# Attention with adaLN and a mixer MLP on one core: scores computed transposed, the MLP put among attention, all engines in a listed order

## The chip, the cores and the metric

One core of one Trainium2 chip. The metric is the device time of one execution in microseconds (us), the slowest core's, of which there is one here. Several executions are timed, and the median is compared.

## What is computed

```python
def reference(A_x, A_k_cache, A_v_cache, A_wq, A_wo, B_x, B_w1, B_w2, B_w3, B_w4, c, w_mod):
    def _A_ref(x, k_cache, v_cache, wq, wo):      # 2048 queries, D = 640, 32 heads of 128, 2048 keys
        q = (x @ wq).reshape(B, Sq, H, Dh).transpose(0, 2, 1, 3)
        scores = jnp.einsum('bhqd,bhkd->bhqk', q, k_cache) * Dh ** (-0.5)
        p = _softmax(scores, axis=-1)
        o = jnp.einsum('bhqk,bhkd->bhqd', p, v_cache)
        return o.transpose(0, 2, 1, 3).reshape(B, Sq, H * Dh) @ wo
    def _B_ref(x, w1, w2, w3, w4):                # F = 1728
        h = _gelu(_layernorm(x) @ w1)
        ...                                       # the four quarters of h shifted by +1, -1, +2, -2 rows: hs
        x1 = x + hs @ w2
        return x1 + _gelu(_layernorm(x1) @ w3) @ w4
    sa, ca, ga, sb, cb, gb = six parts of _silu(c) @ w_mod
    h = _layernorm(x) * (1 + ca) + sa
    x = x + ga * _A_ref(h, ...)
    h = _layernorm(x) * (1 + cb) + sb
    return x + gb * _B_ref(h, ...)
```

All tensors are bfloat16; sums are kept in float32.

## The kernel before

The five engines are called PE (matmul), ACT (activation functions), DVE (elementwise), POOL and SP; SP and POOL also issue DMAs. The kernel is a row of blocks, one after the other. The first (lines 96 to 179) loads `w_mod` and all of `x`, computes the six modulation vectors, normalizes 16 tiles of 128 queries and leaves `hT`, the transposed input of attention.

The second is attention. It runs over heads, and in each head over 16 query tiles; one (head, tile) is a group, 512 in all. PE computes a group's scores in two halves of 1024 keys, queries on the partitions, into `Sps` (L327). DVE scales each half into `negS` in SBUF and takes its row minimum of the negated scores in the same instruction (L371). POOL joins the two minima (L270), and ACT computes exp over 2048 keys with that as bias (L399) into `Pb`. For the product with V the probabilities must stand with keys on the partitions: seven of eight groups are transposed by a DMA from SP (L297), the eighth by PE (L312) with copies by DVE (L363). Six groups later PE multiplies them with V, whose 129th column is ones and yields the row sum (L344). DVE takes its reciprocal (L382), ACT scales (L405), and POOL writes the 128x128 result to `o_scratch` in DRAM (L285). The next head's K tiles are transposed on PE (L228) and its queries projected (L233) as small jobs in fixed slots, with ACT copying out (L241, L244). The order on each engine is that of these loops, and blocking waits on semaphores tie them together.

Behind attention come four blocks in which attention is over: the output projection with the residual and two layer norms (L487 and L525 to L539, `OTj` read back from `o_scratch` by transposing DMAs, L471), the first MLP layer with GELU (L585, L600), the second with a layer norm (L618 to L641), and the third and fourth (L678, L701, L690, L709 to L714). Layer norms take their root on ACT (L435).

Of the kernel before, what the change touches and what calls it, by code (L numbers as in the profile page):

```python
# [1 line left out]

# [4 lines left out]
ACT = mybir.ActivationFunctionType  # L7
BF16 = mybir.dt.bfloat16
F32 = mybir.dt.float32


class Ev:

    def __init__(self, nc, es, name):
        self.sem = es.enter_context(nc.semaphore(name))
        self.n = 0
# [9 lines left out]
        eng.wait_ge(ev.sem, val)  # L26


def bass_adaLN_cond__mha_block_cached__mixer_s_mlp__prompt_kernel(
    nc, A_x, A_k_cache, A_v_cache, A_wq, A_wo, B_x, B_w1, B_w2, B_w3, B_w4, c, w_mod, out,  # L30
):
# [12 lines left out]
    EPS = 1e-5  # L44
    NG = H * NQT
    x2d = A_x[0]
    out2d = out[0]
    HD = D // 2
    NC2 = [(0, 512), (512, D - 512)]

    with ExitStack() as es:
        sb = lambda name, shape, dt: es.enter_context(nc.sbuf_tensor(name, shape, dt))
        ps = lambda name, shape, dt: es.enter_context(nc.psum_tensor(name, shape, dt))
        o_scr = nc.dram_tensor("o_scratch", [NQT, 128, H, DH], BF16)
        ident = sb("ident", [128, 128], BF16)
# [13 lines left out]
        with ExitStack() as esA:  # L69
            sbA = lambda name, shape, dt: esA.enter_context(nc.sbuf_tensor(name, shape, dt))  # L70
            hT = sbA("hT", [128, KT, SQ], BF16)
            with ExitStack() as es0:
                sb0 = lambda name, shape, dt: es0.enter_context(nc.sbuf_tensor(name, shape, dt))
                c_sb = sb0("c_sb", [128, KT], BF16)
                c_f = sb0("c_f", [128, KT], F32)
                s_bc = sb0("s_bc", [128, KT, 128], BF16)
# [3 lines left out]
                st = sb0("st", [128, 2, 12], F32)  # L80
                mv = sb0("mv", [128, 2, 2], F32)
# [3 lines left out]
                hA = sb0("hA", [128, 2, D], BF16)  # L85
                block = es0.enter_context(nc.Block())
# [92 lines left out]
            with ExitStack() as es1:  # L179
# [10 lines left out]
                On = sb1("On", [128, 8, 128], BF16)  # L190
# [3 lines left out]
                rl = sb1("rl", [128, 8], F32)  # L194
# [3 lines left out]
                block = es1.enter_context(nc.Block())  # L198
# [213 lines left out]
        with ExitStack() as es2:  # L412
            sb2 = lambda name, shape, dt: es2.enter_context(nc.sbuf_tensor(name, shape, dt))
            x1 = sb2("x1", [128, NQT, D], BF16)
# [300 lines left out]
                        W(v, e_o, e_o.n)  # L715


# [1 line left out]
_INS = ['A_x', 'A_k_cache', 'A_v_cache', 'A_wq', 'A_wo', 'B_x', 'B_w1', 'B_w2', 'B_w3', 'B_w4', 'c', 'w_mod']  # L719
_OUTS = [((1, 2048, 640), 'bfloat16')]  # L720
# [23 lines left out]
```

## Time and profile before

| | us |
|---|---|
| three timed runs | 2002.43, 2003.85, 2011.81 |
| median | 2003.85 |
| span of the profiled execution | 2008.4 |
| PE busy in it | 1587.3 (79%) |
| DVE busy | 1547.8 (77%) |
| ACT busy | 1374.8 (68%) |
| POOL busy | 662.8 (33%) |

The profiled execution's own device time is not recorded beside its span; the span lies within the three timed runs, and the program has no part before or behind it that the trace shows. Mean granted clock of PE was 0.954 of full speed. In the profile an engine's group of instructions stands with its line, the tile written and the tiles read, the shape, the count, its busy time and mean time, and the idle time of the engine just before these instructions with what ended it. PE's matmuls are pipelined, so a mean of 387 ns for 512 columns is a latency, and rates are read from dense chains.

### The profile page before, as it was taken

To read this page: it belongs to the slowest core of one execution; us is meant where nothing else is said; L and a number is where in the kernel's file an instruction comes from. 1 tells how busy PE (TensorE), PEld (TensorE's weight loads), DVE (VectorE), ACT (ScalarE), POOL (GpSimd) and SP (SyncE) were. 2 spreads that over 40 slices of the span, in tenths; PEclk is the share of its full clock that TensorE was granted. 3 is DMA by queue.
4 is the path that set the end of the run, shared out by engine and by line. 5 is a ranking of instruction groups with operands and counts; after the bars stand their busy time and mean duration, and the time that the engine had idled before them with its cause. 6 is when DMAs were issued, how large, how long until landed. Compare 5 with 4: busy or idle time off the path is not lost. (4 is left out here: it accounts for less than half of the span.)

```text
span 2008.4 us, 39142 instructions
## 1 busy us (share of the span) xinstructions
PE 1587.3 (79%) x14480; PEld 993.0 (49%) x14708; DVE 1547.8 (77%) x3151; ACT 1374.8 (68%) x1428; POOL 662.8 (33%) x1321
## 2 busy tenths in 40 slices
PE   2388888888888888888888888888888469966798
PEld 1145555555555555555555555555555335533344
DVE  5588888898889888888888888888988437737025
ACT  1288888888888888888888888888888401143430
POOL 0224444444444444444444444444443200010000
PEclk7589999999999999999999999999999879989899
DMA  4189999999999989999988989999999775510201
GB/s 150 38 160 201 198 198 199 201 198 195 199 202 204 190 197 199 198 201 199 194 188 191 187 200 196 203 199 196 195 202 196 174 199 122 106 33 1 89 14 40
DMA packets 1044381, 333.95 MB, mean 166 GB/s; under 512 B 1011744, under 2 KB 1024992, under 8 KB 1044192
## 3 DMA queue, kind: packets, MB, share of 16 engines
q1 hardware_dynamic: 1013472, 275.81, 68.3%
q0 software_dynamic: 30720, 55.63, 10.6%
q8 instruction: 118, 1.93, 0.4%
q14 instruction: 71, 0.58, 0.1%
HBM read 60.26 MB, written 19.40 MB: 40 GB/s over the span
## 5 line engine op out<-in xcount | busy, mean ns | idle before, releaser
L371 DVE TENSOR_SCALAR_CACHE_REDUCE negS<-Sps 128x1024 f32<-128x1024 f32 x1024 | 1207.7, 1217 | 168.6 <-PE Sps L327 163.7
L399 ACT ACTIVATE Pb<-negS,nm 128x2048 bf16<-128x2048 f32 x512 | 1025.2, 2003 | 213.9 <-POOL nm L270 194.8
L327 PE MATMUL Sps<-KTs,QT 128*128 128x512 bf16 x1889 | 549.8, 387 | 162.7 <-DVE negS L371 142.2
L270 POOL TENSOR_SCALAR nm<-nm 128x1 f32<-128x1 f32 x512 | 145.3, 284 | 840.9 <-DVE negS L371 840.9
L327 PEld LDWEIGHTS Sps<-KTs,QT 128*128 128x128 bf16 x2048 | 154.3, 98 | 402.8 <-DVE negS L371 320.6
L344 PEld LDWEIGHTS PTp<-Vaug,PTs 128*128 128x128 bf16 x4096 | 263.0, 99 | 66.4 <-issue 24.0
L285 POOL DMA_DIRECT2D o_scratch<-On x512 | 289.3, 565 | 4.5 <-ACT On L405 4.0
L344 PEld LDWEIGHTS Oaug<-Vaug,PTs 128*128 128x128 bf16 x4096 | 259.6, 98 | 59.9 <-issue 1.1
L344 PE MATMUL PTp<-Vaug,PTs 128*128 128x129 bf16 x4096 | 286.9, 223 | 1.5 <-ACT On L405 1.2
L344 PE MATMUL Oaug<-Vaug,PTs 128*128 128x129 bf16 x4096 | 281.4, 220 | 0.0
L487 PE MATMUL Sps<-wo,OTj 128*128 128x128 bf16 (+1 forms) x1008 | 140.9, 301 | 38.6 <-DMA OTj<-o_scratch 37.8
L233 PE MATMUL QPp<-hT,wq 128*128 128x512 bf16 x607 | 155.9, 386 | 5.2 <-ACT QT L244 2.0
L487 PEld LDWEIGHTS Sps<-wo,OTj 128*128 128x128 bf16 x1024 | 80.1, 99 | 100.1 <-DMA OTj<-o_scratch 37.6
L435 ACT ACTIVATE sdB<-mvB 128x1 f32<-128x1 f32 x48 | 9.7, 203 | 158.3 <-DVE mvB L67 158.3
L312 PE MATMUL PTp<-ident,Pb 128*128 128x128 bf16 x1024 | 78.7, 220 | 43.3 <-ACT Pb L399 43.3
L256 POOL DMA_DIRECT2D Vaug<-in_A_v_cache_dram x128 | 104.9, 820 | 5.6 <-issue 5.5
L363 DVE COPY PTs<-PTp 128x1024 bf16<-128x1024 bf16 x128 | 86.8, 678 | 25.4 <-PE PTp L312 25.3
L250 POOL DMA_DIRECT2D Knat<-in_A_k_cache_dram x128 | 104.7, 820 | 0.4 <-issue 0.4
L709 DVE TENSOR_TENSOR t<-Sps,xb 128x640 f32<-128x640 f32 x16 | 13.2, 825 | 103.6 <-PE Sps L690 103.6
L405 ACT ACTIVATE On<-Oaug,rl 128x128 bf16<-128x128 f32 x256 | 89.7, 350 | 2.5 <-DVE rl L382 2.5
L405 ACT ACTIVATE On<-PTp,rl 128x128 bf16<-128x128 f32 x256 | 89.5, 350 | 2.0 <-DVE rl L382 2.0
L312 PEld LDWEIGHTS PTp<-ident,Pb 128*128 128x128 bf16 x1024 | 60.1, 98 | 54.6 <-ACT Pb L399 54.5
(72 smaller groups left out, 1127.6 us busy)
## 6 DMA issues: line engine op xcount, KB each, us to landing
Knat<-in_A_k_cache_dram POOLq DMA_DIRECT2D x128, 128.0 KB, 3.7
Vaug<-in_A_v_cache_dram POOLq DMA_DIRECT2D x128, 128.0 KB, 3.8
o_scratch<-On POOLq DMA_DIRECT2D x512, 32.0 KB, 3.3
PTs<-Pb SPq DMA_TRANSPOSE x448, 4.8
wq<-in_A_wq_dram POOLq DMA_DIRECT2D x32, 160.0 KB, 4.7
wo<-in_A_wo_dram SPq DMA_DIRECT2D x1, 5120.0 KB, 17.0
wmod<-in_w_mod_dram SPq DMA_DIRECT2D x1, 4800.0 KB, 14.8
x_sb<-in_A_x_dram SPq DMA_DIRECT2D x1, 2560.0 KB, 21.3
```

What stands on the lines that cost most here:

```text
L233: ins = t.matmul(QPp[:, 0:512], wq[:, hb, kk, :], hT[:, kk, cc * 512:(cc + 1) * 512], start=(kk == 0), stop=(kk == KT - 1))
L250: e_k[hb][pc // 2].inc(e.dma_start(Knat[:, hb, pc * 4:(pc + 1) * 4, :], A_k_cache[0, h, pc * 512:(pc + 1) * 512, :].rearrange("(t p) d -> ...
L256: e_v[hb].inc(e.dma_start(Vaug[:, hb, q * 4:(q + 1) * 4, 0:128], A_v_cache[0, h, q * 512:(q + 1) * 512, :].rearrange("(t p) d -> p t d", p ...
L270: e_nm.inc(g.tensor_scalar(out=nm[:, r8:r8 + 1], in0=nm0[:, r8:r8 + 1], scalar1=nm1[:, r8:r8 + 1], scalar2=None, op0=ALU.min))
L285: e_od[g_ % 8].inc(g.dma_start(o_scr[jj, :, hh, :], On[:, g_ % 8, :]), 16)
L312: ins = t.transpose(PTp[:, q * 128:(q + 1) * 128], Pb[:, b4, kt * 128:(kt + 1) * 128], ident[:])
L327: ins = t.matmul(Sps[:, col:col + 512], QT[:, hb, j * 128:(j + 1) * 128], KTs[:, hb, col:col + 512], start=True, stop=True)
L344: ins = t.matmul(ob[:, 0:129], PTs[:, b4, kt, :], Vaug[:, hb, kt, 0:129], start=(kt == 0), stop=(kt == NKT - 1))
L371: ins = v.tensor_scalar(out=negS[:, b, half * 1024:(half + 1) * 1024], in0=Sps[:, half * 1024:(half + 1) * 1024], scalar1=-SCALE, scalar2= ...
L399: e_exp.inc(a.activation(Pb[:, b4, :], negS[:, b, :], ACT.Exp, bias=nm[:, r8:r8 + 1], scale=-1.0))
L405: e_nrm.inc(a.activation(On[:, r8, :], OB[g_ % NOB][:, 0:128], ACT.Copy, scale=rl[:, r8:r8 + 1]))
L487: ins = t.matmul(YB[b][:, c0:c0 + cw], OTj[:, jj % 3, hh, :], wo[:, hh, c0:c0 + cw], start=(hh == 0), stop=(hh == H - 1))
```

## The change

The kernel is written anew as a list of operations (`fast_path`), each with an engine, a supposed duration, a priority and the tiles that it reads and writes. `Plan.schedule` puts them in order by a list scheduler with these durations: of those that can start soonest on an engine (within 30 ns) it takes the one with the lowest priority number. `Plan.emit` writes out the order with semaphore waits. The durations do not know of table loads of ACT, which are put into the program afterwards wherever the next function is not in the loaded set.

The queries are cut into 4 chunks of 512. The outer loop runs over chunks, the inner over 32 heads; one (chunk, head) is a step, 128 in all. In a step the scores are computed transposed, keys on the partitions and 512 queries along the row, two key tiles to one PSUM tile `S` of 1024 columns, of which there are two. ACT computes exp from PSUM without a maximum, straight into `PT`, which is already the operand that PV needs. PV accumulates four query tiles in two PSUM banks, `O0` and `O1`, one tile of each. DVE normalizes into `On`, and every four heads four small transposing DMAs and eight matmul groups add the output projection into `y_t`. K is loaded from DRAM by a transposing DMA. The MLP of a chunk (`phase_b`) is put among the steps of the next chunk; that of the last chunk comes behind everything. All small products share two PSUM tiles `M`. At the end the reciprocals of the row sums are compared with two bounds; if one is outside, the old kernel (`general_path`, word for word the one before) runs as well.

```diff
+    def schedule(self):
...
+                lim = min(st)[0] + 30.0
+                c = min((x for x in st if x[0] <= lim), key=lambda x: x[1:3])
+                if best is None or c[0] < best[0]:
+                    best = c
...
+def fast_path(nc, es, flag, A_x, A_k_cache, A_v_cache, A_wq, A_wo, B_w1, B_w2, B_w3, B_w4, c, w_mod, out):
...
+    S_ps = [ps("S%d" % i, [128, 1024]) for i in range(2)]
+    O_ps = [ps("O%d" % i, [128, 512]) for i in range(2)]
+    M_ps = [ps("M%d" % i, [128, 512]) for i in range(2)]
...
+    EXPSET = "natural_log_exp_and_others"
+    P.op("ACT", lambda e: e.preload_act_table_set(EXPSET), 1300, (), (), -200)
+
+    def back_to_exp(g, prio):
+        o = P.op("ACT", lambda e: e.preload_act_table_set(EXPSET), 1300, (), (), prio, after=tuple(g))
+        return (o,)
...
+    def ln(src, src_tiles, prio):
...
+        P.op("ACT", lambda e: e.activation(rs[i].ap, mv[i][:, 1:2], ACT.Ln, bias=EPS), 220, (mv[i],), (rs[i],), prio - 50)
+        P.op("ACT", lambda e: e.activation(rs[i].ap, rs[i].ap, ACT.Exp, scale=-0.5), 220, (rs[i],), (rs[i],), prio - 50)
...
+    def step(ch, h):
+        s = ch * H + h
+        k, v, w, q = KTs[s % 2], V[s % 2], wq[s % 2], QT[s % 2]
...
+        dma("SP", lambda e: e.dma_start_transpose(k.ap.unsqueeze(1), A_k_cache[0, h]), 700, (), (k,), lp)
+        dma("POOL", lambda e: e.dma_start(w.ap, A_wq[:, h * 128:(h + 1) * 128].rearrange("(k p) d -> p k d", p=128)), 160, (), (w,), lp - 0.5)
+        dma("POOL", lambda e: e.dma_start(v[:, :, 0:128], A_v_cache[0, h].rearrange("(t p) d -> p t d", p=128)), 512, (), (v,), lp + 0.2)
...
+        P.op("PE", qp, KT * MM(QC), (w,) + tuple(hT[ch % 2]), (m,), s - 1.8)
...
+        for j in range(NKT // 2):
...
+            P.op("PE", smm, 2 * MM(QC), (k, q), (sp,), s + j / 8 - 1.0)
+            last_exp[s, j] = P.op("ACT", lambda e, sp=sp, pt=pt: e.activation(
+                pt.ap.rearrange("p k q -> p (k q)"), sp.ap, ACT.Exp, scale=SCALE), 1040, (sp,), (pt,), s + j / 8,
+                after=gate.pop((s, j), ()))
+            for b in range(2):
...
+                P.op("PE", pv, 4 * 59, (pt, v), (o[b],), s + j / 8 - 0.9 + b * 0.01, accum=True)
...
+    def phase_b(ch):
...
+        X1, X2 = base + 5, base + 13
+        a1 = () if last else (lambda: last_exp[X1, 7],)
...
+            P.op("PE", mm, KT * MM(QC), (WA,) + tuple(nT[0:4]), (m,), X1 - 1, after=a1)
+            for (p0, p1, dl) in segs[n]:
+                g1.append(P.op("ACT", lambda e, m=m, n=n, p0=p0, p1=p1, dl=dl: e.activation(
+                    us_t[p0:p1, n, 128 + dl:640 + dl], m[p0:p1, :], GELU), act(QC), (m,), (us,), X1 - 2, after=a1))
+        if not last:
+            gate[X1 + 1, 0] = back_to_exp(g1, X1 - 2)
...
+            plan.schedule()
+            plan.emit(nc, es, {"SP": 24, "POOL": 12})
+        redo = nc.values_load(flag[0:1, 0:1])
+        with nc.If(redo > 0):
+            general_path(nc, A_x, A_k_cache, A_v_cache, A_wq, A_wo, B_x, B_w1, B_w2, B_w3, B_w4, c, w_mod, out)
```

PE, in the middle of attention. Before, a group's four score matmuls (L327) alternate with 16 matmuls of PV of an earlier group (L344, into `PTp` or `Oaug` in turn), with eight transposes (L312) now and then:

```order
L344 MATMUL Oaug<-Vaug,PTs 128x129 x16
L327 MATMUL Sps<-KTs,QT 128x512 x4
L344 MATMUL PTp<-Vaug,PTs 128x129 x16
L312 MATMUL PTp<-ident,Pb 128x128 x8
L327 MATMUL Sps<-KTs,QT 128x512 x4
```

After, at a change of step in a stretch without output projection (L470 is PV, L458 the scores, L446 the q projection of the step after next):

```order
L470 MATMUL f_O<-f_V,f_PT 128x129 x8
L458 MATMUL f_S<-f_QT,f_KTs 128x512 x2
L446 MATMUL f_M<-f_hT,f_wq 128x512 x5
L470 MATMUL f_O<-f_V,f_PT 128x129 x8
L458 MATMUL f_S<-f_QT,f_KTs 128x512 x4
L470 MATMUL f_O<-f_V,f_PT 128x129 x16
L458 MATMUL f_S<-f_QT,f_KTs 128x512 x2
L470 MATMUL f_O<-f_V,f_PT 128x129 x8
L458 MATMUL f_S<-f_QT,f_KTs 128x512 x2
```

The eight PV matmuls of a pair now stand directly ahead of the score matmuls of the pair two further on, and each PV waits for its own exp.

ACT, at the first MLP layer. Before, this layer's GELUs (L600) stood in a block of their own, behind one table load:

```order
L600 ACT_TABLE_LOAD
L600 ACTIVATE us<-Sps 128x512
L600 ACTIVATE us<-Sps 32x512 x2
L600 ACTIVATE us<-Sps 64x512 x3
L600 ACTIVATE us<-Sps 96x512
```

After, in each of the first three chunks (L461 is the exp of attention, L569 the GELU):

```order
L461 ACTIVATE f_PT<-f_S 128x1024 x13
L569 ACT_TABLE_LOAD
L569 ACTIVATE f_us<-f_M 128x512
L569 ACTIVATE f_us<-f_M 32x512
L461 ACT_TABLE_LOAD
L461 ACTIVATE f_PT<-f_S 128x1024
L569 ACT_TABLE_LOAD
L569 ACTIVATE f_us<-f_M 32x512
L461 ACT_TABLE_LOAD
L461 ACTIVATE f_PT<-f_S 128x1024
L569 ACT_TABLE_LOAD
L569 ACTIVATE f_us<-f_M 64x512
```

It goes on like this to the ninth GELU: the gate holds back pair 0 of the next step only, and its pairs 1 to 7 pass between the GELUs through the other `S` tile, with 16 table loads in all.

ACT, in the second MLP layer of the last chunk, behind all attention. Before, one load served the roots of all layer norms (L435), with copies (L448) between:

```order
L435 ACT_TABLE_LOAD
L435 ACTIVATE sdB<-mvB 128x1 x2
L448 COPY nT<-Oaug 128x5x128
L435 ACTIVATE sdB<-mvB 128x1
L448 COPY nT<-QPp 128x5x128
```

After (L355 is the logarithm, L356 the exp that makes it a reciprocal root):

```order
L569 ACTIVATE f_us<-f_M 128x512
L355 ACT_TABLE_LOAD
L355 ACTIVATE f_rs<-f_mv 128x1
L356 ACT_TABLE_LOAD
L356 ACTIVATE f_rs<-f_rs 128x1
```

There each of the two small functions has a load of its own, ten for five tiles.

More of the change, by code (lines that the diff above doesn't have):

```diff
@@ L1 @@
 from contextlib import ExitStack
+import heapq
 import concourse.bass as bass
@@ L9, with __init__, __getitem__ @@
 F32 = mybir.dt.float32
+I32 = mybir.dt.int32
+class Op:
+    def __init__(self, eng, fn, dur, lat, prio, dma, kb):
+        self.eng, self.fn, self.dur, self.lat, self.prio, self.dma, self.kb = eng, fn, dur, lat, prio, dma, kb
+        self.deps = {}
+        self.order = set()
+        self.newps = None
+        self.ptiles = ()
+        self.succ = []
+        self.ready = 0.0
+        self.needed = False
+        self.sem = self.semval = self.prev_dma = None
+class Tile:
+    def __init__(self, ap=None, pool=None):
+        self.ap, self.pool = ap, pool
+        self.writer = []
+        self.readers = []
+        self.refs = []
+        self.bank = None
+    def __getitem__(self, k):
+        return self.ap[k]
```

534 lines of the change are left out of this document (533 added, 1 removed).

## Prediction

> **What bounds the kernel now.** I read the table of stages first, because the shares of the whole span mix stages with different limits.
>
> ```profile
> 100.00:1600.00 1500.00, 1230.67 (x12194) 805.95 (x12385) 1307.31 (x2688) 1267.27 (x1213) 642.31 (x1298) 0.98 0.96 194
> 1600.00:1640.00 40.00, 15.19 (x82) 7.51 (x85) 3.50 (x7) 0.20 (x1) 0.00 (x0) 0.62 0.95 264
> 1640.00:1760.00 120.00, 119.31 (x909) 69.45 (x921) 88.21 (x176) 14.47 (x40) 0.00 (x0) 1.00 0.54 111
> 1760.00:1860.00 100.00, 62.65 (x432) 33.83 (x436) 53.45 (x119) 37.48 (x74) 8.65 (x1) 0.91 0.06 17
> 1860.00:2008.00 148.00, 129.67 (x719) 61.46 (x733) 41.03 (x53) 36.16 (x60) 0.00 (x0) 0.95 0.14 48
> ```
>
> The columns are the stretch, its length, then busy time with counts of PE, PEld, DVE, ACT and POOL, the granted clock, the DMA share and GB/s. About 100 us are start-up, 1500 us attention, and 408 us the output projection and MLP, which run alone. In attention DVE is busy 1307 of 1500 us, and ACT, PE and the DMA engines stand close behind. The groups by line say on what:
>
> ```profile
> L371 DVE TENSOR_SCALAR_CACHE_REDUCE negS<-Sps 128x1024 f32<-128x1024 f32 x1024 | 1207.7, 1217 | 168.6 <-PE Sps L327 163.7 <-ACT Pb L399 2.6
> L371 DVE DVE_READ_ACCUMULATOR negS<-Sps 128x1 f32 x1024 | 85.0, 83 | 0.0
> L399 ACT ACTIVATE Pb<-negS,nm 128x2048 bf16<-128x2048 f32 x512 | 1025.2, 2003 | 213.9 <-POOL nm L270 194.8
> L363 DVE COPY PTs<-PTp 128x1024 bf16<-128x1024 bf16 x128 | 86.8, 678 | 25.4 <-PE PTp L312 25.3
> ```
>
> One group is 128 queries of one head. Its two score halves cost DVE 2 x (1.217 + 0.083) = 2.60 us, and an eighth of the groups adds two 0.678 us copies, 0.17 on average. So the max pass on DVE sets the pace, and 512 groups in some 1520 us are 2.97 us each, or 11.9 us for the 512 queries that the changed kernel calls a step.
>
> **What goes.** The max pass, the POOL minimum behind it, the PE and DMA transposes of the probabilities and the trip of O through DRAM all go. With them goes the DVE bound, so the question is what comes next. A step is now 8 pairs of key tiles. Each pair has two score matmuls, one exp of 128x1024 straight from PSUM, and 8 PV matmuls.
>
> **The step if PE alone counted.** Back-to-back rates come from the dense chains at the end:
>
> ```profile
> 1884.67 10.96 PE Sps L678 x49
> 1940.25 8.29 PE Sps L690 x55
> 801.29 1.10 PE L344 MATMUL Oaug<-Vaug,PTs 128*128 128x129 bf16 x16
> ```
>
> A 512-column matmul takes 10.96/49 = 0.224 us. The second row alternates 512 and 128 columns, 8.29/55 = 0.151 us each, so a mean of 320 columns, the new width, is 0.151. Sixteen PV matmuls span 1.10 us with the last one's 0.22 of latency, so (1.10 - 0.22)/15 = 0.0587. Per step: q projection 5 x 0.224 = 1.12, scores 16 x 0.224 = 3.58, PV 64 x 0.0587 = 3.76, output projection 8 x 0.151 = 1.21, together 9.67 us. Times 128 steps that is 1238 us, the lower bound.
>
> **The step as ordered.** PE's order is PV of pair j, scores of pair j+2, PV of j+1, and so on, since S has only two tiles. PV j waits for exp j, and the scores of j+2 stand behind that PV. So there is a loop: exp, hand-over to PE, PV, scores, hand-over to ACT. Its pieces:
>
> ```profile
> 801.91 1.22 DVE L371 TENSOR_SCALAR_CACHE_REDUCE negS<-Sps 128x1024 f32<-128x1024 f32 x1
> 802.67 1.14 PE L327 MATMUL Sps<-KTs,QT 128*128 128x512 bf16 x4
> 803.12 0.35 ACT L405 ACTIVATE On<-PTp,rl 128x128 bf16<-128x128 f32 x1
> 803.39 1.23 DVE L371 TENSOR_SCALAR_CACHE_REDUCE negS<-Sps 128x1024 f32<-128x1024 f32 x1 [0.17 <-PE Sps L327]
> 803.64 1.10 PE L344 MATMUL PTp<-Vaug,PTs 128*128 128x129 bf16 x16
> ...
> L241 ACT COPY KTs<-QPp 128x1024 bf16<-128x1024 bf16 x64 | 64.6, 1009 | 7.6 <-PE QPp L228 7.6
> L244 ACT CAST QT<-QPp 128x512 bf16<-128x512 f32 x128 | 73.4, 573 | 9.6 <-PE QPp L233 9.6
> L701 ACT ACTIVATE gT<-Sps 128x512 bf16<-128x512 f32 x52 | 31.0, 597 | 35.3 <-PE Sps L678 35.3
> ```
>
> The exp from PSUM is not in the trace. Without a bias operand ACT takes 0.573 for 512 columns and 1.009 for 1024, so 0.85 ns a column; a GELU of 512 is 0.597, hence 1.01 to 1.04 for 1024, and I take 1.02. ACT ends at 803.12 + 0.35 = 803.47 and the waiting PV starts at 803.64: 0.17. Eight PV matmuls are 0.47. Scores start at 802.67 and their reader at 803.39: 0.72. The loop is 1.02 + 0.17 + 0.47 + 0.72 = 2.38 us and carries two pairs, so 1.19 us a pair and 9.5 us a step. ACT alone would need 8 x 1.02 = 8.2, and PE's share of this is 7.3, so neither is full: **the latency loop over two score tiles binds.**
>
> The other PE work is slipped in. A q projection, 1.12 us, stands ahead of the first PV of a step and beside the wait for the O bank (two reciprocals and two multiplies on DVE, about 1.3 us, so covered). Following it through the pairs, both ACT slots run dry once, and the step grows from 9.5 to 10.7. Two output projections of 0.60 us a step cost between 0 (they fall into PE's 1.19 - 0.92 = 0.27 us idle per pair) and 0.60; I take 0.30, near the middle, since idle per pair covers half. That gives 11.3 us a step, **1446 us for 128** (bounds 1238 and, with every insert added in full and O late by 0.3, 1530).
>
> **MLP among attention, chunks 0 to 2.** The planner's order on ACT interleaves the seven later GELUs of the first MLP layer singly with exps, and each change needs a table load: 16 loads where two would do.
>
> ```profile
> 1789.42 1.28 ACT L600 ACT_TABLE_LOAD   x1 [10.15 <-PE Sps L585]
> 1790.71 9.43 ACT L600 ACTIVATE us<-Sps 128x512 bf16<-128x512 f32 x16
> ```
>
> A load takes 1.28 us and the GELU follows at once; 16 GELUs take 9.43, so 0.59 each. The block is 16 x 1.28 + 9 x 0.59 + 7 x 1.02 = 33.0 us. Behind it PE must first wait for the gated exp (1.02 + 0.17) and run the 56 + 8 PV matmuls held up (3.76), one projection (0.60) and scores (0.72) before ACT gets new work: 6.3. The 39.3 us hold 9 pairs worth 9 x 1.41 = 12.7, so 26.6 extra, **80 us for three chunks** (planned as two loads it would be some 9 each).
> The Trainium skill, page "ScalarE: Activation LUTs", section "What ACT_TABLE_LOAD costs", puts a switch at about 2.66 us, because a drain of about 1.38 goes with the load; by that the three blocks would be 48 x 1.38 = 66 us longer. Here the load follows 10.15 us of idling, so the row cannot show a drain ahead of it.
>
> The third layer is contiguous: 70 x 0.224 = 15.7 twice, 12.6 for the shorter chunk 0, plus 2.5 each for the load back, the first exp and the hand-over: 50. The fourth: 22 inserts of 14 x 0.151 = 2.11, of which the idle hides 0.3: 40. The second: 22 of 0.755, less the same: 11. Layer norms put two small ACT instructions into the loop 47 times, and their DVE work delays some releases of O:
>
> ```profile
> L435 ACT ACTIVATE sdB<-mvB 128x1 f32<-128x1 f32 x48 | 9.7, 203 | 158.3 <-DVE mvB L67 158.3
> L64 DVE BATCH_NORM_STATS2 stB<-xb 128x6 f32<-128x320 f32 x32 | 15.8, 495 | 1.1
> L65 DVE BATCH_NORM_STATS2 stB<-xb 128x6 f32<-128x320 f32 x32 | 15.2, 476 | 0.0
> L67 DVE BATCH_NORM_AGGREGATE mvB<-stB 128x2 f32<-128x12 f32 x48 | 10.0, 209 | 1.7
> L531 DVE SCALAR_TENSOR_TENSOR tmpB<-x,mvB,mod_bc 128x640 f32<-128x640 bf16 x16 | 14.2, 885 | 0.6
> L528 DVE TENSOR_TENSOR x<-tmpB,x_sbB 128x640 bf16<-128x640 f32 x16 | 13.2, 825 | 0.5
> L539 DVE TENSOR_SCALAR nrmB<-xb,mvB,rstdB 128x640 bf16<-128x640 f32 x16 | 9.8, 614 | 0.6
> ```
>
> 47 x 2 x 0.20 = 19 on ACT; with the DVE delays I take 25 (bounds 0 and 45).
>
> **Loads.** K now comes transposed from DRAM, one per step on SP, and V, wq and wo on POOL.
>
> ```profile
> q1 hardware_dynamic: 1013472, 275.81, 68.3%
> q0 software_dynamic: 30720, 55.63, 10.6%
> PTs<-Pb SPq DMA_TRANSPOSE x448, 4.8
> OTj<-o_scratch SPq DMA_TRANSPOSE x16, 6.8
> w<-in_B_w_dram SPq DMA_DIRECT2D x2, 800.0 KB, 6.1
> c_sb<-in_c_dram SPq DMA_DIRECT2D x1, 1.2 KB, 3.0
> ```
>
> Transposes move 275.81 MB / (0.683 x 2008.4 us) = 201 GB/s, the software queue 261. Per step: K 0.52 MB 2.6 us, O 0.13 MB 0.65, V, wq and wo 0.85 MB 3.2, so 6.5 of 11.3 us against a share of 0.96 before. K of step s+2 is asked for when the scores of s are done and must land one step later; the same 512 KB land in 4.8 us now. I cost it at nothing; the cover is a whole step. On POOL a load of V can stand behind 2 MB of MLP weights, 8 us at 261 GB/s, four times a chunk; with a step of cover I take 0 (bounds 0 and 12).
>
> **Both ends.** Start: c lands at 3, the first 800 KB near 7, two modulation parts, four tiles of 2 x 0.885 + 1.18 on DVE, transposes, q and scores: the first exp at about 30. After the last exp only chunk 3's MLP is left: O to SBUF and its transposes 6; projection tail 2; four tiles of 7.2 us on DVE (0.82 + 1.65 + 2 x 1.18 + 1.77 + 0.61), 29; transpose 3.3; first layer paced by nine GELUs, 7.7; second layer with five layer norms, each with two table loads (2 x 1.28 + 0.40 = 2.96), 19; transpose 3.3; third 140 x 0.151 + 0.5 = 21.5; fourth 21; last tile and store 4; the flag 2: 119.
>
> **Sum.** 30 + 1446 + 80 + 50 + 40 + 11 + 25 + 119 = 1801, so 1800 against a span of 2008.4. The median of the runs is 2003.85, 0.2% below that span, so I use the sum unchanged.
>
> **Rivals.**
> PE dense. If inserts fill the loop's idle time, attention is 1238 and layer norms are free: 30 + 1238 + 80 + 50 + 46 + 17 + 119 = 1580. For it: PE has other work in most pairs. Against: PV j cannot be moved ahead of its exp, and 20 of 32 pairs hold no insert.
> Dear table switches. If a switch also has to empty and refill ACT, at an estimate as much again as the load, the 48 loads of the blocks and the 10 of the tail cost 58 x 1.28 = 74 more: 1875. For it: in the row above nothing ran ahead of the load. Against: another load stands 0.02 us behind an ACTIVATE:
>
> ```profile
> 3.71 0.21 ACT L113 ACTIVATE c_f<-c_sb 128x5 f32<-128x5 bf16 x1 [1.69 <-DMA c_sb<-in_c_dram]
> 3.94 1.28 ACT L123 ACT_TABLE_LOAD   x1
> ```
>
> That is the rule of the Trainium skill's page "ScalarE: Activation LUTs"; its 1.38 us would give 1801 + 80 = 1881, and the 0.02 us does not agree with it.
> Late K, the slower side. If the transposing load of 2048 DRAM rows takes longer than a step, each step lasts as long as that load: 355 us of other terms + 128 x L. It passes 2008 at L = 12.9 us, 2.7 times the 4.8 of the row; at 16 us it gives 2403. For it: neither row has K's shape. Against: both move 256-byte pieces at 201 GB/s, and 1 MB from DRAM lands in 6.8.
> It does not do what it says: the guard fires and the old path runs behind the new one, 1801 + 2004 = 3805. With 2048 keys and small scores, one over the row sum is near 2 to the -11, far inside the bounds of 2 to the +-30.
>
> **How the numbers follow.** Chances: forecast 0.67 (1640 to 1860), PE dense 0.15, dear switches 0.11 (1860 to 1950), late K 0.05 of which 0.04 past 2008, guard 0.01, other 0.01. The range 1600 to 1930 leaves out most of the dense case's lower half and the late K. A measurement of this kernel tells about 0.5% from no change: faster 0.94, same 0.02, slower 0.04.
>
> **What would show it.** Right: exps near 1.02 us; in a stretch of plain attention 11.3 us a step with PE some 85% busy and its idle time put down to ACT's exp; 67 table loads, 16 in each of three blocks of about 33 us; K landing in under 8 us; 119 us after the last exp. Wrong: PE above 95% (dense), gaps of over 1 us beside loads, PE or PEld waiting for K's DMA, or a step far from 11.3, since 0.5 us there is 64 us in all.

## The result, and the profile after

| | us |
|---|---|
| before, median of 4 runs | 2005.65 (2002.43 to 2011.81) |
| after, median of 4 runs | 1690.46 (1681.23 to 1704.16) |
| after / before | 0.8425, 95% interval 0.838 to 0.8471 |
| predicted | 1800 (1600 to 1930), sum of terms 1801 |
| profiled execution after | 1693.83, its span 1689.8 |

The kernel became 315 us faster; 204 was forecast. Medians in this section and below are of all runs of a kernel, while the ratios (to the kernel before) with intervals leave out executions that were disturbed on the chip, so the two can stand a per cent apart.

First the table of stages of the kernel after, for the long middle, a plain stretch of four steps without MLP, and the end (stretch, length, busy time of PE, PEld, DVE, ACT, POOL, granted clock, DMA share, GB/s):

```profile
100.00:1500.00 1400.00, 1268.78 (x11438) 794.07 (x11436) 461.86 (x1088) 1018.31 (x1133) 272.73 (x279) 0.96 0.71 146
268.50:308.40 39.90, 38.24 (x376) 25.00 (x373) 11.17 (x28) 31.12 (x33) 8.89 (x9) 1.00 0.68 152
1570.00:1690.00 120.00, 64.42 (x396) 35.87 (x396) 53.20 (x112) 38.47 (x76) 1.13 (x1) 0.81 0.17 44
```

DVE, which was busy 1307 of 1500 us before, is now busy 462 of 1400: its bound is gone, as forecast, and the DMA share fell from 0.96 to 0.71. (The share adds up the times of packets, which overlap where it stands above 1 below.) A plain step takes 39.9/4 = 9.98 us, not 11.3. The groups by line, with the idle time ahead of each group and what ended it:

```profile
L461 ACT ACTIVATE f_PT<-f_S 128x1024 bf16<-128x1024 f32 x1024 | 1000.1, 1021 | 388.3 <-PE f_S L458 384.6 <-PE f_O L470 2.8
L470 PE MATMUL f_O<-f_V,f_PT 128*128 128x129 bf16 x8192 | 625.4, 221 | 55.8 <-ACT f_PT L461 45.8 <-DMA f_V<-in_A_v_cache_dram 3.3 <-DVE f_On L481 2.8
L458 PE MATMUL f_S<-f_QT,f_KTs 128*128 128x512 bf16 x2048 | 593.9, 385 | 57.0 <-ACT f_PT L461 40.7 <-DMA f_KTs<-in_A_k_cache_dram 15.9
L569 ACT ACT_TABLE_LOAD x25 | 32.1, 1283 | 0.4
```

The exp takes 1.021 us (1.02 forecast). ACT waits for scores and PE for exps: the mark of a loop between the two. The 25 loads for GELUs had 0.4 us of idling ahead of them in all. There are 67 loads in the whole trace, as forecast, and the three blocks with 16 each take 34.8 us on ACT (33 forecast). K lands on time but for waits of PE of 15.9 us in total.

The loop itself, in order of time, PE and ACT in a stretch without inserts (start, duration, idle time in brackets):

```profile
284.29 0.63 PE L470 MATMUL f_O<-f_V,f_PT 128*128 128x129 bf16 x8
284.48 1.94 ACT L461 ACTIVATE f_PT<-f_S 128x1024 bf16<-128x1024 f32 x2 [0.24 <-PE f_S L458]
284.76 0.59 PE L458 MATMUL f_S<-f_QT,f_KTs 128*128 128x512 bf16 x2
285.56 0.63 PE L470 MATMUL f_O<-f_V,f_PT 128*128 128x129 bf16 x8 [0.20 <-ACT f_PT L461]
286.02 0.59 PE L458 MATMUL f_S<-f_QT,f_KTs 128*128 128x512 bf16 x2
286.47 0.63 PE L470 MATMUL f_O<-f_V,f_PT 128*128 128x129 bf16 x8
286.65 1.94 ACT L461 ACTIVATE f_PT<-f_S 128x1024 bf16<-128x1024 f32 x2 [0.24 <-PE f_S L458]
```

An exp starts at 284.48 and ends at 285.50; its PV starts at 285.56, the scores behind it at 286.02, and the exp of these scores at 286.65. So the loop is 1.02 + 0.06 + 0.46 + 0.63 = 2.17 us for two pairs, where 1.02 + 0.17 + 0.47 + 0.72 = 2.38 was forecast. The two exps of a row of 1.94 start 0.92 apart. The Trainium skill, page "ScalarE: Activation LUTs", section "What ACT_TABLE_LOAD costs", says that neighbouring ACTIVATEs overlap by about 93 ns; 2 x 1.021 - 1.94 = 0.10 us agrees.

All terms, read from the starts and ends of the 1024 exps in the trace (a step is 8 of them; "extra" is a step's length above 9.98):

| term | forecast | after |
|---|---|---|
| to the first exp | 30 | 44.5 |
| 128 plain steps | 1446 | 1277 |
| first-layer blocks, extra in steps 5 to 7 of chunks 1 to 3 | 80 | 90.3 |
| third layer, extra in step 13 | 50 | 46.4 |
| fourth and second layer, layer norms | 76 | 112.0 |
| behind the last exp | 119 | 119.6 |
| sum | 1801 | 1689.8 |

### The profile page after: what moved, and what is told of

The parts are those of the page before. It is cut to its first block, busy times and chain, and to the rows that moved or that the text cites. A ratio compares the mean times of both kernels' runs of the same rounds, so it can differ in the third digit from the quotient of the medians.

```text
span 1689.8 us, 30083 instructions
## 1 busy us (share of the span) xinstructions
PE 1467.7 (87%) x13043; PEld 914.0 (54%) x13043; DVE 574.6 (34%) x1334; ACT 1162.1 (69%) x1330; POOL 308.6 (18%) x322
## 4 chain that ended last, share of the span: by engine, by line
PE 68%; ACT 17%; DMA 7%; DVE 4%; issue 2%; SPq 1%
PE f_O L470 25%; PE f_S L458 20%; ACT f_PT L461 12%; PE f_M L446 8%; PE f_M L501 7%; PE f_M L630 4%; PE f_M L610 3%; DMA f_OT<-f_On 3%; DMA f_KTs<-in_A_k_cache_dram 2%; ACT L569 2%; ACT L461 2%; SPq L439 1%; ACT f_us L569 1%; PE f_M L585 1%; DMA f_nT<-f_nrm 1%
## 5 line engine op out<-in xcount | busy, mean ns | idle before, releaser
L461 ACT ACTIVATE f_PT<-f_S 128x1024 bf16<-128x1024 f32 x1024 | 1000.1, 1021 | 388.3 <-PE f_S L458 384.6
L470 PEld LDWEIGHTS f_O<-f_V,f_PT 128*128 128x128 bf16 x8192 | 514.9, 98 | 297.9 <-ACT f_PT L461 197.0
L470 PE MATMUL f_O<-f_V,f_PT 128*128 128x129 bf16 x8192 | 625.4, 221 | 55.8 <-ACT f_PT L461 45.8
L458 PE MATMUL f_S<-f_QT,f_KTs 128*128 128x512 bf16 x2048 | 593.9, 385 | 57.0 <-ACT f_PT L461 40.7
L441 POOL DMA_DIRECT2D f_V<-in_A_v_cache_dram x128 | 149.6, 1169 | 666.2 <-PE f_O L470 420.8
L458 PEld LDWEIGHTS f_S<-f_QT,f_KTs 128*128 128x128 bf16 x2048 | 164.0, 97 | 118.6 <-ACT f_PT L461 64.4
L501 PE MATMUL f_M<-f_wo,f_OT 128*128 128x320 bf16 x1024 | 182.8, 306 | 12.4 <-DMA f_OT<-f_On 9.4
L509 DVE TENSOR_TENSOR f_yacc<-f_M,f_yacc 128x320 f32<-128x320 f32 x224 | 109.3, 489 | 246.0 <-PE f_M L501 244.8
L440 POOL DMA_DIRECT2D f_wq<-in_A_wq_dram x128 | 110.9, 867 | 396.6 <-PE f_O L470 349.8
L446 PE MATMUL f_M<-f_hT,f_wq 128*128 128x512 bf16 x640 | 163.0, 387 | 2.2 <-ACT f_hT L394 0.8
L446 PEld LDWEIGHTS f_M<-f_hT,f_wq 128*128 128x128 bf16 x640 | 62.4, 99 | 80.8 <-issue 6.5
L614 ACT ACTIVATE f_gT<-f_M 128x512 bf16<-128x512 f32 (+3 forms) x70 | 35.5, 511 | 31.4 <-PE f_M L610 31.3
L355 ACT ACTIVATE f_rs<-f_mv 128x1 f32<-128x1 f32 x64 | 12.1, 201 | 52.3 <-DVE f_mv L354 51.9
## 6 DMA issues: line engine op xcount, KB each, us to landing
f_WA<-in_B_w_dram POOLq DMA_DIRECT2D x4, 2080.0 KB, 10.5
```

The lines of the kernel that those rows point to most:

```text
L440: dma("POOL", lambda e: e.dma_start(w.ap, A_wq[:, h * 128:(h + 1) * 128].rearrange("(k p) d -> p k d", p=128)), 160, (), (w,), lp - 0.5)
L441: dma("POOL", lambda e: e.dma_start(v[:, :, 0:128], A_v_cache[0, h].rearrange("(t p) d -> p t d", p=128)), 512, (), (v,), lp + 0.2)
L446: ins = e.matmul(m.ap, w[:, kk, :], hT_t[ch % 2][:, kk, :], start=(kk == 0), stop=(kk == KT - 1))
L458: ins = e.matmul(sp[:, r * QC:(r + 1) * QC], k[:, kt * 128:(kt + 1) * 128], q.ap, start=True, stop=True)
L461: last_exp[s, j] = P.op("ACT", lambda e, sp=sp, pt=pt: e.activation(pt.ap.rearrange("p k q -> p (k q)"), sp.ap, ACT.Exp, scale=SCALE), 104 ...
L470: ins = e.matmul(o[b][:, u * 129:u * 129 + 129], pt[:, r, qt * 128:(qt + 1) * 128], v[:, kt, 0:129], start=(kt == 0 and u == 0), stop=(kt ...
```

## The experiments

Each kernel is the one after with the edit shown. The question that matters most: is the plain step of 9.98 us PE's own work (the dense rival) or the loop? PE's share in the stretch above, 38.24 of 39.90, does not tell. Busy matmuls include their latency: one PV is busy 0.22 us, where the next job starts 0.46 us after the first of eight. By the median spacing of matmuls in the trace (PV 0.057, 512 columns 0.2155, 320 columns 0.136), PE's work in a step is 64 x 0.057 + 21 x 0.2155 + 8 x 0.136 = 9.26 us (written as 9.27 and 9.3 in the expectations), 93% of the step.

**Half the exp (e1_exp_half).** The exp of every second key tile is left out, that half of `PT` being cleared once at the start:

```diff
-                pt.ap.rearrange("p k q -> p (k q)"), sp.ap, ACT.Exp, scale=SCALE), 1040,
+                pt.ap[:, 0, :], sp[:, 0:QC], ACT.Exp, scale=SCALE), 1040,
```

> Leaves out the exp of the second key tile of every pair (512 of 1024 columns; the other half of PT is set to zero once), so the result differs; PE's instructions and every engine's order stay. Plain steps of the changed kernel repeat at 39.9 us per four, 9.98 us each. Theory A (PE nearly full: 64 x 0.057 + 21 x 0.2155 + 8 x 0.136 = 9.27 us of pure streaming, ACT only just behind): a step falls at most to 9.3, and attention ends below 100 us earlier in all. Theory B (the loop exp, PV, scores binds as forecast, 2.18 us for two pairs): the loop shrinks by 0.43 to 1.75, below PE's two-pair work of 1.78, so each gap of it closes and a step falls by over 1 us if the inserts stay additive. Theory C (PE is the only bound and the 0.7 us over 9.27 are fixed bubbles elsewhere, at O's hand-over or semaphores): the step stays at 9.8 or more.

One run, 1641.31 us. Its plain stretch in the table of stages:

```profile
258.80:296.40 37.60, 37.34 (x376) 25.27 (x374) 11.18 (x28) 18.56 (x32) 8.90 (x9) 1.00 0.79 162
```

The plain step is 37.6/4 = 9.40 us, the exp 0.596. This fits theory A, and not the fall of over 1 us of B or the 9.8 of C. Shortening the exp by 0.42 us takes 0.58 from a step, where a loop that always binds would give 4 x 0.42 = 1.7 and a dense PE nothing: the reading is that the loop binds down to PE's own 9.26 and then PE does. The spans differ by 50 and not by 128 x 0.58 = 74, since the first exp came 10 us later (POOL clears the buffers ahead of part of its loads), the first chunk's steps took 13 more (the third of them 22.6, with PE waiting for K) and the end 3; the three MLPs among the steps took 3 less.

**Scores first (e7_scores_first).** The direct test, one number: a higher rank puts the scores of pair j+2 ahead of the PV of pair j, so that PV is out of the loop.

```diff
-            P.op("PE", smm, 2 * MM(QC), (k, q), (sp,), s + j / 8 - 1.0)
+            P.op("PE", smm, 2 * MM(QC), (k, q), (sp,), s + j / 8 - 1.3)
```

> The scores of pair j+2 stand ahead of the PV of pair j in PE's row; the amount of work is unchanged. Loop theory (the part of the plain step above PE's 9.3 us comes from exp, hand-over, PV, scores, hand-over over two score tiles, 2.18 us per two pairs): without the PV the loop is 1.02 + 0.06 + 0.63 = 1.71 us, below PE's own 1.77 for two pairs, so the plain step falls from 9.98 to 9.3 to 9.5 us, and the kernel takes 60 to 85 us less than 1690, 1605 to 1630. Rival, PE dense (the step is PE's work plus fixed hand-overs, whatever stands first): the step stays at 9.8 or more, and the time within 20 us of 1690. Rival, the O bank (PV of a new step waits for DVE): the step keeps a gap of over 0.3 us at its first PV and falls by less than 0.3 us.

1586.29 us, ratio 0.7877 (0.783 to 0.7924): 104 us less by medians, more than expected. Four plain steps of this kernel, first its row of the table of stages, then a piece of the same stretch in order of time:

```profile
235.20:272.40 37.20, 36.83 (x368) 25.95 (x373) 11.37 (x29) 30.81 (x32) 8.93 (x10) 1.00 0.79 164
...
243.65 3.03 ACT L461 ACTIVATE f_PT<-f_S 128x1024 bf16<-128x1024 f32 x3
243.79 0.28 PE L470 MATMUL f_O<-f_V,f_PT 128*128 128x129 bf16 x2
243.91 0.59 PE L458 MATMUL f_S<-f_QT,f_KTs 128*128 128x512 bf16 x2
244.34 0.85 PE L470 MATMUL f_O<-f_V,f_PT 128*128 128x129 bf16 x12
245.03 0.59 PE L458 MATMUL f_S<-f_QT,f_KTs 128*128 128x512 bf16 x2
```

37.2/4 = 9.30 us a step, PE's 9.26 within 0.04, and no wait of PE for another engine. The PV between two score jobs is now already at hand (x12, x2) instead of just arriving. The loop theory holds, and both rivals fall. Of the 110.5 us between the two spans (1689.8 and 1579.3), 128 x 0.68 = 87 come from plain steps; 27 more come from the MLP's steps, less 3 at the ends.

**Both exps behind a GELU block gated (e2_gate_both).** Only the first exp of the step behind the block waited for the block's table load back, so the second S tile's exps slipped between the GELUs.

```diff
-            gate[X1 + 1, 0] = back_to_exp(g1, X1 - 2)
+            gate[X1 + 1, 0] = gate[X1 + 1, 1] = back_to_exp(g1, X1 - 2)
```

> Gates pairs 0 and 1 of the step behind the first MLP layer instead of pair 0 alone, so both S tiles are held and the nine GELUs stay together: 2 table loads a block in place of 16. Measured now, the steps 5 to 7 of a chunk take 30 us more than three plain ones. Theory A (the loads are the cost of the block): 14 x 1.28 = 18 us less per chunk, and up to 21, so 54 to 63 us in all: 1627 to 1636 us. Theory B (the block is held by PE's first layer, its two M tiles and the PV backlog, and loads run in time that ACT has to spare): under 20 us in all, above 1670.

1651.87 us, ratio 0.824 (0.818 to 0.83): above A's 1627 to 1636, and well under B's 1670. The first-layer blocks fell from 90.3 us extra to 17.8 + 15.1 + 14.0 = 46.9. The block of the first of them, on ACT, after (start only) and with the gate:

```profile
429.79 1.28 ACT L461 ACT_TABLE_LOAD   x1
431.08 1.02 ACT L461 ACTIVATE f_PT<-f_S 128x1024 bf16<-128x1024 f32 x1
432.12 1.28 ACT L569 ACT_TABLE_LOAD   x1
433.42 0.59 ACT L569 ACTIVATE f_us<-f_M 32x512 bf16<-32x512 f32 x1
434.01 1.28 ACT L461 ACT_TABLE_LOAD   x1
```

```profile
425.72 1.28 ACT L569 ACT_TABLE_LOAD   x1
427.01 0.60 ACT L569 ACTIVATE f_us<-f_M 128x512 bf16<-128x512 f32 x1
428.96 1.80 ACT L569 ACTIVATE f_us<-f_M 32x512 bf16<-32x512 f32 x3 [1.35 <-PE f_M L565]
```

The 42 loads saved in three blocks are worth 43.4 us, 1.03 each, less than a load's 1.28, because GELUs then wait for their matmuls (1.35 us) instead. In the trace of after a round is 432.12 to 436.35, 4.23 us for 1.28 + 0.59 + 1.28 + 1.02 = 4.17: a switch costs its load and some 0.03. ACT stands idle for 0.02 us or less ahead of every load but the program's first. The drain of about 1.38 us that the Trainium skill, page "ScalarE: Activation LUTs", section "What ACT_TABLE_LOAD costs", adds to a load is not there in any of the 67.

**The start (e4_start).** All four x tiles of the first chunk are loaded ahead of `w_mod` and K, with a fourth buffer. In the kernel after, x tile 2 stood on SP behind two K loads. SP's row in order of time, the first 22 us in the table of stages, and the line of K's issues with its shortest, median and longest in ns:

```profile
3.34 21.84 SPq L439 DMA_TRANSPOSE f_KTs<-in_A_k_cache_dram  x2
25.23 0.58 SPq L309 DMA_DIRECT2D f_xin<-in_A_x_dram  x1
...
3.00:25.00 22.00, 7.12 (x30) 3.58 (x30) 8.49 (x18) 2.40 (x7) 8.79 (x11) 1.00 1.08 277
...
L439 SPq DMA_TRANSPOSE f_KTs<-in_A_k_cache_dram x128: 1236/2450/17514, 3.3 to 1551.2; - x128
```

These two issues held SP for 21.84 us, one of them for 17.5, where the median is 2.45. Nothing had to be waited for, but the DMA engines were full (share 1.08) with V, wq, wo and MLP weights of POOL's queue.

```diff
-    first_x = [load_x(j, -99 + j) for j in range(2)]
+    first_x = [load_x(j, -99 + j / 8) for j in range(4)]
```

> Loads all four x tiles of the first chunk ahead of w_mod and K (a ring of four in place of three); nothing else is changed on purpose. Now SP is held 21.8 us by its first two transposing loads of K while x tiles 2 and 3 wait behind them, and the first exp comes at 44.5 us. Theory A (that order is what delays the start): first exp at 30 to 36 us, and the total 9 to 14 us less. Theory B (the DMA engines are full with 10 MB of prefetch until 35 us and K itself lands late): first exp above 40 us, total unchanged within 4 us.

1699.29 us, ratio 0.8461 (0.8408 to 0.8514): no change. The first exp came at 36.7 us, 8 earlier, and the first nine steps together took 15 more. PE's row of this kernel, and DVE's around the wait:

```profile
56.26 1.55 PE L331 MATMUL f_M<-f_WB,f_s_bc 128*128 128x320 bf16 x10 [0.29 <-DVE f_mod L334]
62.13 4.43 PE L446 MATMUL f_M<-f_hT,f_wq 128*128 128x512 bf16 x10 [4.32 <-DVE f_mod L334]
...
60.70 0.89 DVE L374 SCALAR_TENSOR_TENSOR f_hA<-f_tmp,f_rs,f_mod 128x640 bf16<-128x640 f32 x1
61.50 0.88 DVE L334 TENSOR_SCALAR f_mod<-f_M 128x320 f32<-128x320 f32 x2
```

The next q projection waits for an M tile, whose reader on DVE (the copy of a modulation vector, L334) stands behind layer norms of the next chunk. So the first exp came close to theory A's 30 to 36, the total as in B, and neither had named this wait, which is 4.3 of the 15 us; the others were not taken apart.

**The MLP apart (e6_mlp_apart).** How much does it bring to put the MLP among attention? Here each chunk's MLP runs by itself: the scores of the next chunk's first heads (and its first projections) are listed behind the MLP's last operations, and the gates go.

```diff
-            P.op("PE", smm, 2 * MM(QC), (k, q), (sp,), s + j / 8 - 1.0)
+            P.op("PE", smm, 2 * MM(QC), (k, q), (sp,), s + j / 8 - 1.0, after=tuple(mlp_end) if h < 4 else ())
...
-        a1 = () if last else (lambda: last_exp[X1, 7],)
+        a1 = ()
```

> Undoes one part of the change: the MLP of a chunk runs alone before the next chunk's scores start, as the last chunk's does. Now the three interleaved MLPs cost 249 us beyond 128 plain steps, and the one that runs alone costs 119.6 us from the last exp to the end. If interleaving hides what it should, this kernel pays about 100 + 115 + 115 = 330 in place of 249, so 1760 to 1780 us with plain steps unchanged at 9.98. If the interleaving gains nothing (table loads and gates give back what it hides), it stays within 15 us of 1690.

One run, 1742.18 us: between the two. A chunk's MLP alone takes 96 to 105 us above a step; the steps' extra sums to 297 us against 249 interleaved. So only 48 us were hidden, but the 42 loads between GELUs and exps, which are gone here, are part of why: in e2_gate_both, interleaved without them, the extra is 188, and 109 us are hidden. That is more than PE's idle time in 96 plain steps, 96 x (9.98 - 9.26) = 69 us, so that time alone did not set what could be hidden.

**Combinations.** Do the gains add? Scores first, both exps gated, and one table load in place of ten in the tail (e8_all); the same with an earlier start, modulation parts held back to steps 14 to 17 (e9_all_start):

```diff
+        else:
+            back_to_exp(g1, X1 - 2)
```

> Scores first, both exps behind the GELU block gated (2 table loads a block), and the tail's GELUs in one run (no exp table between them). If the three costs are apart from each other, the gains add: about 39 us for the gate (1690 to 1652 in its own run), 60 to 85 for the order, 9 loads of 1.28 = 11.5 in the tail: 1555 to 1580. If they are the same idle time seen twice (PE's lower clock behind the blocks being the same in each), 1600 or more.

> As the one before, with all four x tiles loaded ahead of the modulation weights and K, and the four later modulation parts not before steps 14 to 17. Theory: the earlier start of the x tiles alone was given back in steps 1 to 5 because PE stood in its row behind modulation matmuls whose 800 KB weights were still on their way; without them in front, the first exp at about 37 us stays a gain of 6 to 10 us over the kernel with the same other edits. Rival: the first steps wait for K, V and wq themselves (all DMA engines busy to 35 us or more), and the gain is under 4 us.

They do not. e8_all: 1608.09 us, ratio 0.7985 (0.7947 to 0.8023), slower than scores first alone, the "1600 or more" of its expectation; e9_all_start: 1622.32, ratio 0.7976 (0.7931 to 0.8021), the same as e8_all, so the gain was under 4 us, as the rival said. The first exp came at 42.3 us, only 3.3 earlier than in e8_all. In the profile of e9_all_start steps 17 and 18, right behind the loads of the parts that were held back, take 21.9 and 34.5 us, with PE waiting for K; this profile is of an execution of 1648.27 us, 26 above the median, so whether the shorter ones have these waits is not known. In e8_all two places stand out, a step of 32.5 us (two stages, then PE) and one of 36.0 (ACT):

```profile
446.00:460.00 14.00, 13.84 (x146) 10.03 (x147) 6.44 (x17) 12.37 (x19) 3.93 (x4) 1.00 1.09 230
460.00:474.00 14.00, 5.05 (x40) 3.13 (x38) 2.58 (x7) 0.92 (x1) 2.04 (x2) 0.77 1.29 75
...
471.80 4.45 PE L501 MATMUL f_M<-f_wo,f_OT 128*128 128x320 bf16 x16 [8.95 <-DMA f_OT<-f_On]
483.54 1.89 PE L458 MATMUL f_S<-f_QT,f_KTs 128*128 128x512 bf16 x4 [5.42 <-DMA f_KTs<-in_A_k_cache_dram]
...
519.32 1.28 ACT L616 ACT_TABLE_LOAD   x1
520.61 0.49 ACT L616 ACTIVATE f_gT<-f_M 128x384 bf16<-128x384 f32 x1
521.12 1.28 ACT L461 ACT_TABLE_LOAD   x1
```

In the first the DMA engines are full for 40 us from the moment at which POOL asks for 2.08 MB of fourth-layer weights (446.13), and O's transposes and K, behind each other on SP, land late. K was also asked for late: its issue waited for PE, which was itself waiting for O's transposes (SP's waits from 455 to 490 us: total, times, longest):

```profile
SPq L439 <- PE f_M L501: 12.1, 1, 12.1
```

In the second the third layer's GELUs alternate with exps, as the first layer's did. To split the two: the third layer gated too (e13_gates), a third K buffer asked for a step earlier with nothing else but scores first (e12_k3), and all together (e11_k3_gates).

```diff
-            gate[X2 + 1, 0] = back_to_exp(g2, X2 - 2)
+            gate[X2 + 1, 0] = gate[X2 + 1, 1] = back_to_exp(g2, X2 - 2)
```

```diff
-    KTs = ring("KTs", 2, [128, SK], BF16)
+    KTs = ring("KTs", 3, [128, SK], BF16)
...
-        dma("SP", lambda e: e.dma_start_transpose(k.ap.unsqueeze(1), A_k_cache[0, h]), 700, (), (k,), lp)
+        dma("SP", lambda e: e.dma_start_transpose(k.ap.unsqueeze(1), A_k_cache[0, h]), 700, (), (k,), lp - 1 if s > 2 else lp)
```

> Scores first with both gates at both blocks and the tail's GELUs in one run, two K buffers as before. With e12_k3 this splits the combination: if the alternating third-layer block was the main loss, this comes to 1560 to 1585; if late K was, it stays at 1595 to 1615 with PE waiting for K for 20 us or more.

> Scores first and a third K buffer, nothing else. If late K costs time in this order, PE's waits for K vanish and the time falls by those waits, 10 to 25 us below 1586; if K is on time but for a wait or two, it stays within 10 us. The plain step stays at 9.30 in both cases.

> Scores first, both gates at both GELU blocks, the tail's GELUs in one run, and a third K buffer asked for a step earlier. Theory: the gates lost in the combination before because of two things that are not the gates: the third layer's GELUs alternated with exps in one chunk (36.0 us for one step), and K, held up on SP's queue behind 2 to 3 MB of MLP weights, came late (steps of 32.5 and 26.2 us). With both removed the gain of the gates in the first-layer blocks (5 to 9 us each) and the loads stays: 1545 to 1570. Rival: a faster attention leaves no idle time for the MLP at all, its work is paid in full wherever it stands, and the time stays within 15 us of 1586.

| | us, median | ratio | interval | PE's wait for K at L458 |
|---|---|---|---|---|
| scores first | 1586.29 | 0.7877 | 0.783 to 0.7924 | 21.1 |
| with all gates (e13_gates) | 1598.41 | 0.7941 | 0.7914 to 0.7968 | 30.5 |
| with third K (e12_k3) | 1563.2 | 0.7687 | 0.7648 to 0.7727 | 6.8 |
| with both (e11_k3_gates) | 1550.83 | 0.7704 | 0.7674 to 0.7733 | 2.9 |

e13_gates came out as its second case said, so late K was the main loss. The third buffer alone is worth 0.7877 - 0.7687 = 0.019 of 2010, 38 us by ratios, 23 by medians (its expectation had 10 to 25) and 16 between the two profiles, of which that of e12_k3 is of an execution of 1564.87 us; PE's direct waits for K fell by 14. The gates without it are worth nothing. But with it the gates brought nothing either: the ratios of the last two rows cannot be told apart. So e11_k3_gates came into its expected range (1545 to 1570), but the theory behind it, that the gates' gain would show once K was on time, fell. ACT's row of e11_k3_gates tells why:

```profile
400.10 1.28 ACT L569 ACT_TABLE_LOAD   x1
414.99 0.60 ACT L569 ACTIVATE f_us<-f_M 128x512 bf16<-128x512 f32 x1 [13.60 <-PE f_M L565]
```

The GELU block was entered 13.6 us before the transposed input nT was there, and no exp could run meanwhile. So the block goes one step later (e14_later_block):

```diff
-        X1, X2 = base + 5, base + 13
+        X1, X2 = base + 6, base + 13
```

> As e11_k3_gates, with the first layer's GELU block one step later (6 steps behind the chunk's end instead of 5). Theory: in e11_k3_gates the GELU table was loaded 13.6 us before the block's input (nT, transposed on SP behind K) had come, and both gated exps left PE without work meanwhile; a step later the input is there, so the first-layer blocks fall from 31.3, 31.2 and 24.6 us extra to 14 to 20 each, and the time from 1551 to 1510 to 1535. Rival: the input is late because SP's queue is full whatever the step, the 13 us idle stretch moves along with the block, and the time stays within 10 us of 1551.

1546.24 us, ratio 0.7633 (0.76 to 0.7666): above the 1510 to 1535 of the theory. The blocks did what the theory said and more: counted over steps 5 to 8, so that the shifted block is whole, 8.8, 10.5 and 9.4 us extra in place of 31.3, 30.5 and 24.5. But of these 58 us all but 11 were given back in later steps. The groups by line name the place, PE's two main ones in this kernel:

```profile
L470 PE MATMUL f_O<-f_V,f_PT 128*128 128x129 bf16 x8192 | 623.2, 221 | 24.8 <-DMA f_V<-in_A_v_cache_dram 22.3 <-DVE f_On L481 0.3
L458 PE MATMUL f_S<-f_QT,f_KTs 128*128 128x512 bf16 x1865 | 565.7, 379 | 31.6 <-DMA f_KTs<-in_A_k_cache_dram 11.7 <-ACT f_PT L461 9.9 <-issue 1.6
```

So V gets a third buffer as well and is asked for a step earlier, and `PT` gets 7 in place of 8 to make room (e15_v3):

```diff
-    V = ring("V", 2, [128, NKT, 130], BF16)
+    V = ring("V", 3, [128, NKT, 130], BF16)
...
-    NPT = 8
+    NPT = 7
```

> As e14_later_block with a third V buffer too, asked for a step earlier, and 7 buffers of the exps' output in place of 8 to make room. In e14_later_block PE waited 22.3 us for V and 11.7 us for K behind the MLP weights. Theory: what the later block gained was given back to those transfers, and with a step more of cover PE's waits for V fall below 8 us and the time by 12 to 25 us, 1515 to 1532. Rival: the transfers are late because the DMA engines are full in those stretches, an earlier request only moves the wait to K or to the output transposes, and the time stays within 8 us of 1546.

PE's same two groups:

```profile
L470 PE MATMUL f_O<-f_V,f_PT 128*128 128x129 bf16 x8192 | 635.3, 220 | 0.8 <-DVE f_On L481 0.6
L458 PE MATMUL f_S<-f_QT,f_KTs 128*128 128x512 bf16 x2048 | 608.7, 379 | 13.1 <-DMA f_KTs<-in_A_k_cache_dram 10.3 <-ACT f_PT L461 2.3 <-DVE f_QT L449 0.3
```

1515.07 us, ratio 0.7514 (0.7475 to 0.7553): the waits for V are gone, those for K stay near 10 us, and the theory holds. This version beats both kernels: 10.8% less than the kernel after (0.7514/0.8425). Its span is 1506.3 us: 49.5 to the first exp, 128 x 9.275 = 1187, 150 of MLP among the steps, and 119.5 behind the last exp. It was not run without the gates, so what they are worth in it is not shown.

## Why the prediction came out as it did

**What bounds before, and what goes:** right as far as the profiles show. DVE was the busiest engine of attention before, and nothing took its place there: after, it is busy for 34% of the span. No run changed the kernel before, to test its bound.

**The step as ordered:** the mechanism was right, and this is the term whose size failed. "The latency loop over two score tiles binds" is what scores first showed, and ACT's and PE's waits name it. But it bound by little, 9.98 over PE's 9.26. The step was put at 11.3 us and is 9.98, 169 us over 128 steps. Two parts make it up. The loop is 2.17 to 2.18 us and not 2.38: the hand-over of 0.17 was taken from a PV behind a short PSUM copy and is 0.06 here, and 0.72, from a start of four score matmuls to DVE, is 0.63 from a start of two to ACT; that is 4 x 0.2 = 0.8 us a step. The inserts cost 9.98 - 4 x 2.18 = 1.26 us a step, where 11.3 - 4 x 2.38 = 1.78 was taken. More of them must fall into PE's idle time than was assumed; which of them do was not taken apart.

**The dense rival:** wrong for this order, and its own figure was too high. The spacing taken from the chains at the end gave 9.67 us; the measured 9.26 comes from 0.136 in place of 0.151 for 320 columns, 0.2155 in place of 0.224, and 0.057 in place of 0.0587. The chains had been divided with pauses and the last matmul's latency (0.39 us) in them; the median spacing in the same trace of before is 0.216 for L678, and 0.216 and 0.056 for L690's two widths, a mean of 0.136. The sign named for this rival, "PE above 95%", showed (95.8% in the plain stretch), and that for the forecast, "some 85% busy", did not, although the loop bound; a busy share made of latencies was no sign at all. Moving one job in PE's row was.

**First-layer blocks:** 80 forecast, 90.3 measured, the loads of 1.28 and their count right. The first of the three on ACT, from its first load to its last, and ACT's next steady work:

```profile
425.95 1.28 ACT L569 ACT_TABLE_LOAD   x1
...
459.43 1.28 ACT L292 ACT_TABLE_LOAD   x1
...
467.19 1.94 ACT L461 ACTIVATE f_PT<-f_S 128x1024 bf16<-128x1024 f32 x2 [3.15 <-PE f_S L458]
```

The block takes 34.8 us and not 33.0 (1.35 of it a wait for matmuls), and 6.5 pass behind it, where 6.3 was forecast. The 9 pairs in it are worth 9 x 9.98/8 = 11.2 and not 12.7, because the step was priced too high. That makes 30 extra in place of 26.6, so over 4 of the 10 us missed in the three blocks are the step's own error again.

**The remark "planned as two loads it would be some 9 each":** 15.6 each with the gate alone, 8.8 to 10.5 where the input was on time too.

**Second and fourth layer, layer norms:** 76 forecast, 112 measured. The fourth and second by the measured spacing are 22 x (14 x 0.136 + 5 x 0.136) = 57. In the other 55 are PE's waits for K (15.9), for O's transposes (9.4) and for V (3.3), 28.6 together. The 26 left stand where 25 was forecast for layer norms, but these were not tried apart. Two small slips of the sum offset each other: the third layer's pieces add up to 51.5 and not 50, the second's to 10 and not 11.

**Loads:** K in under 8 us was right in the median (4.6), and costing the loads at nothing left out the 28.6 us of waits above, of 1690. In faster orders of the same kernel late K and V became a large loss, as the runs with third buffers show.

**Both ends:** behind the last exp 119 forecast, 119.6 measured, so close in part by luck: the first layer's matmuls began 34 us behind that exp, where 40 was forecast, and what follows took 85, where some 79 was. The start was 14.5 us too short, because it priced the transfers as if each had the queue to itself; SP's issues of K took 21.8 us, and 7.8 of the 14.5 went when x came ahead of them (e4_start).

**The other rivals:** dear table switches did not occur (0.03 us besides the load), K was not late by steps, and the guard did not fire. Of the 169 us by which the steps were too long, the start (14.5), the second and fourth layers with layer norms and late transfers (36) and the blocks (10) took back 61, and the third layer gave 4. So the time fell 110 under the forecast, inside the range, and would have been further off without errors of the other sign.

## What to carry to other kernels

In a loop between two engines over two buffers, put ahead of the waiting job what refills the other engine's buffer, and let the job that merely consumes follow: here one rank in a list was worth about 5% of the old time. Read whether an engine is full from the spacing of its instructions and not from a busy share that holds latencies. And after each gain look again at transfers that were on time: the gates, worth 39 us alone, brought nothing on top of the new order, while a third buffer brought 38 us there for K (by ratios) and 31 for V in the last version (by medians).

## What the runs showed of the hardware

A DMA transpose of K is cheap in the median (issue 2.45 us, 4.6 us to land), but with the DMA engines full its issue held SP for up to 17.5 us, and everything behind it on SP waited, small loads too. Full engines moved very different amounts: 75 GB/s at a share of 1.29 in e8_all, 277 at 1.08 at the start of the kernel after. A table load of ACT takes 1.283 us and, with its neighbours, some 0.03 besides. In the first-layer block, where PE waits for ACT again and again, its granted clock is lower as well: 0.69 in the kernel after, with PE busy for 22.02 of 38 us. Five matmuls of that layer take 2.31 us there at 438.29, and 1.25 at 427.90. In the same block of e14_later_block, in the 13 us around it, PE is busy for 12.25 and the clock is 1.00. The two rows, the kernel after first:

```profile
424.00:462.00 38.00, 22.02 (x87) 7.27 (x85) 4.04 (x9) 35.74 (x35) 1.15 (x1) 0.69 0.20 44
...
409.00:422.00 13.00, 12.25 (x95) 7.08 (x95) 2.58 (x7) 10.93 (x15) 2.03 (x2) 1.00 0.64 102
```
